# A state-space scan with a gated feed-forward: tokens dealt four to a partition, and a changed order of the first loads and turns

## The chip, the cores and the metric

The kernel runs on one core of a Trainium2 chip. The metric is the device time of one execution in microseconds. A core has five engines with queues of their own: TensorE (PE, matrix products; PEld is its weight load), VectorE (DVE), ScalarE (ACT), GpSimd (POOL) and SyncE (SP), which here only issues transfers.

## The reference

`x` is 2048 tokens of 512 channels, bf16. It is normalised once, and two branches read the result; their product is added to `x`:

```python
xn = _layernorm(x, axis=-1)
# branch A: a diagonal complex recurrence over the tokens
Bu = einsum("bld,pd->blp", xn, ((Lam_bar - 1) / Lam)[:, None] * Bmat)
h  = Lam_bar * h + Bu[:, t, :]                      # for t in 0..2047
s  = 2 * einsum("blp,dp->bld", hseq, Cmat).real + xn * Dskip
# branch B
g  = silu((gelu(xn @ w_gate) * (xn @ w_up)) @ w_down)   # 512 -> 1376 -> 512
return x + s * g
```

## The kernel before, in words

**Tiles.** The tokens are worked in four slabs (`s`) of 512 (`TS`), each of four tiles (`m`) of 128 tokens. Tile `m` of slab `s` holds the tokens `s*512 + m*128 + p`, one to a partition `p` (L195: `x_r`). A slab's `x` comes in one transfer (`load_slab`, L216), but slab 0 comes tile by tile (`load_x`, L221).

**A slab's work.** The normalised tokens `xna` are transposed by a DMA into `xnT`, which has channels on partitions and tokens along the free side. `gate_tile` (L421) makes the products with `w_up` and `w_gate` from it (weights 1376 wide, in three pieces `CH` of 512, 512 and 352), `at_t` turns the gated result by a DMA into `atT`, and `down_pair` (L456) multiplies by `w_down`. `half` (L522) runs the recurrence for half of the states: eight groups of four products give `Bu` in PSUM, ACT copies each into `U` (L534), DVE turns it into a rotating frame (L544), scans along the tokens (L563) and turns back into `hst`, the states in order of time. `y_tile` (L500) multiplies `hst` (as weights, 128 tokens at a time, L482) by `C`, and DVE multiplies by the gate, adds `x` and writes `ot`; SP sends it out in rows (L498). Six PSUM banks (`ring`) go round, two more (`ybank`) serve the turns at the head and the last products.

**The head, slab 0.** Here PE turns tiles 0 to 3 itself, not a DMA. For tile 0 the sum of each token is shared by ACT (L339, the last 128 channels) and DVE (L341, the first 384), DVE subtracts the mean (L343), PE turns it in two pairs (L313), and DVE (L319) and ACT (L321) copy one pair each into `W`, which serves as `xcT`. Tiles 1 to 3 are summed by ACT (L347), centered by DVE (L348), turned by PE (`head_t`, L328) and copied whole by DVE (L330). PE needs `ident` and two little parameter turns too (L588, L589; DVE copies them out in L591). Then come the products with `w_up`, `up_rows(m, k)` (L376): for tile `m` and row block `k` of 128 channels, two products of 128x512, added up over `k` in two banks. The scale of each token (`rs`) is applied when ACT evacuates them (L392). `dummies` (L293) are seven products of constants at the start, `fill(1, 0)` (L299, called in L648) is one more, placed ahead of tile 1's turn.

**Order.** Every step is added to a list by `Plan.add` with what it reads and writes; `ORDER` (L21) is a list of step numbers, written out, and `Plan.run` emits the steps in that order, so it sets the order on each engine's queue. The figures given with a step (cost, landing, rank) don't reach the chip. SP's queue begins with tiles 0, 1 and 2 of `x`, then the row blocks 0, 1 and 2 of `w_up` (the first 1024 columns), tile 3, row block 3, the rest of `w_up`, and `w_gate` (L225 to L234). PE's order at the head is: dummies, turn of tile 0, parameters, filler, turn of tile 1, `up_rows(0,0)`, turn of tile 2, `up_rows(1,0)` and so on.

Of the kernel before, what the change touches and what calls it, by code (L numbers as in the profile page):

```python
# [10 lines left out]
AF = mybir.ActivationFunctionType  # L11
# [7 lines left out]


ORDER = (  # L21
    20, 21, 22, 23, 24, 0, 26, 25, 19, 17, 18, 16, 1, 39, 14, 15, 12, 13, 2, 41, 3, 4, 5, 27, 28, 29, 30, 33, 60, 32, 46, 45, 40, 61, 34, 31, 63, 42,
    65, 62, 64, 69, 68, 66, 67, 70, 71, 72, 73, 35, 36, 37, 50, 51, 52, 54, 48, 53, 49, 57, 56, 58, 137, 38, 6, 43, 44, 147, 7, 79, 76, 82, 74, 80,
    77, 81, 78, 75, 8, 95, 91, 85, 97, 86, 93, 87, 88, 92, 55, 84, 47, 138, 94, 83, 96, 198, 149, 199, 151, 135, 59, 98, 136, 153, 9, 103, 107, 99,
    101, 109, 111, 104, 119, 100, 115, 102, 117, 108, 110, 125, 123, 133, 131, 216, 220, 139, 217, 140, 106, 120, 90, 112, 127, 214, 221, 105, 116,
    134, 154, 218, 150, 113, 126, 118, 124, 89, 215, 114, 128, 219, 122, 141, 148, 121, 143, 222, 223, 129, 130, 142, 152, 10, 11, 155, 160, 164, 179,
    162, 166, 181, 161, 183, 165, 224, 163, 185, 227, 167, 226, 225, 180, 182, 358, 186, 184, 229, 144, 168, 169, 170, 172, 171, 173, 174, 175, 176,
    177, 178, 187, 156, 132, 233, 234, 158, 237, 238, 157, 235, 228, 241, 243, 258, 275, 283, 280, 279, 276, 282, 244, 259, 236, 277, 278, 281, 284,
    285, 159, 239, 245, 296, 264, 247, 240, 246, 292, 260, 242, 200, 201, 202, 265, 302, 262, 297, 311, 293, 261, 298, 248, 303, 317, 307, 204, 188,
    203, 205, 263, 300, 294, 312, 308, 322, 299, 301, 315, 326, 313, 295, 309, 189, 191, 286, 190, 192, 230, 206, 207, 208, 318, 352, 316, 330, 332,  # L30
    232, 231, 305, 304, 327, 341, 209, 210, 211, 310, 324, 314, 328, 331, 323, 337, 290, 325, 339, 345, 287, 329, 288, 289, 333, 146, 320, 193, 212,
    195, 196, 213, 197, 353, 347, 359, 319, 194, 335, 334, 354, 364, 365, 343, 338, 145, 346, 340, 342, 360, 249, 250, 355, 366, 254, 306, 418, 426,
    291, 376, 380, 378, 393, 377, 381, 344, 382, 397, 394, 348, 395, 410, 420, 379, 383, 398, 421, 425, 419, 396, 424, 411, 349, 350, 361, 253, 252,
    369, 251, 256, 257, 357, 266, 267, 336, 414, 435, 415, 370, 436, 375, 255, 321, 356, 362, 351, 416, 443, 450, 412, 444, 423, 417, 445, 399, 422,
    413, 441, 439, 451, 446, 460, 458, 400, 440, 454, 437, 461, 442, 456, 481, 455, 475, 427, 269, 428, 429, 432, 438, 452, 471, 430, 465, 459, 479,
    371, 453, 433, 457, 271, 270, 268, 448, 480, 482, 502, 473, 273, 274, 466, 500, 272, 367, 363, 431, 447, 476, 463, 503, 472, 492, 496, 462, 372,
    486, 493, 501, 497, 474, 373, 484, 384, 385, 388, 386, 387, 467, 368, 434, 537, 477, 523, 494, 519, 478, 498, 487, 495, 524, 499, 525, 526, 520,
    507, 483, 389, 468, 390, 488, 374, 489, 504, 391, 505, 392, 401, 402, 403, 405, 406, 449, 551, 539, 521, 508, 552, 522, 513, 514, 535, 538, 536,
    515, 509, 404, 408, 407, 409, 527, 528, 531, 530, 518, 532, 469, 485, 464, 553, 490, 506, 557, 555, 541, 558, 569, 563, 556, 540, 559, 542, 554,
    565, 561, 567, 564, 578, 619, 562, 560, 574, 570, 624, 625, 576, 620, 584, 575, 568, 566, 580, 577, 591, 585, 599, 582, 589, 583, 597, 579, 593,  # L40
    581, 595, 572, 598, 600, 614, 510, 529, 516, 533, 571, 491, 587, 621, 629, 630, 612, 511, 622, 586, 626, 635, 615, 594, 596, 610, 608, 592, 590,
    604, 606, 636, 613, 607, 609, 605, 611, 534, 543, 544, 617, 601, 545, 573, 517, 627, 512, 602, 631, 470, 649, 616, 547, 548, 546, 549, 550, 637,
    623, 588, 643, 641, 644, 603, 645, 628, 638, 632, 618, 647, 650, 648, 655, 656, 642, 651, 661, 662, 646, 666, 667, 671, 672, 639, 640, 633, 634,
    652, 657, 658, 663, 664, 668, 669, 673, 674, 653, 654, 659, 660, 665, 670, 675,
)


# [33 lines left out]
def kernel(  # L81
# [109 lines left out]
    def dma(eng, issue, land, emit, reads=(), writes=(), **kw):  # L191
        return pl.add(eng, issue, emit, reads, writes, lag=land, **kw)

    TURN, SLAB = (3, 2.28, 1.5), (2, 1.5, 1.0)
    x_r = A_x[0].rearrange("(m p) d -> p m d", p=P)  # L195
    out_td = out[0]
    w_of = {
        "wg": (wg, B_w_gate.rearrange("(k p) f -> p k f", p=P)),
        "wu": (wu, B_w_up.rearrange("(k p) f -> p k f", p=P)),
# [14 lines left out]
               [(nm, k, c) for k in range(k0, k1) for c in range(3) if c0 <= CH[c][0] < c1])  # L214

    def load_slab(s, **kw):  # L216
        dma(SP, 0.8, 4.0, lambda: nc.sync.dma_start(out=x_tok[:, s * M : (s + 1) * M, :], in_=x_r[:, s * M : (s + 1) * M, :]),
            writes=[("x", s, m) for m in range(M)], svc=SLAB, **kw)


    def load_x(m, end, landed):  # L221
        dma_sp(end, landed, lambda: nc.sync.dma_start(out=x_tok[:, m, :], in_=x_r[:, m, :]), [("x", 0, m)])

    W2 = CH[1][1]
    load_x(0, 1.12, 2.92)  # L225
    load_x(1, 1.59, 3.35)
    load_x(2, 2.06, 3.75)
    load_w("wu", 0, 1, 0, W2, 2.53, 5.1)
    load_w("wu", 1, 2, 0, W2, 3.0, 6.3)
    load_w("wu", 2, 3, 0, W2, 3.5, 7.4)  # L230
    load_x(3, 4.0, 7.75)
    load_w("wu", 3, 4, 0, W2, 4.5, 8.7)
    load_w("wu", 0, KT, W2, F, 5.0, 9.9)
    load_w("wg", 0, KT, 0, F, 5.6, 13.7)  # L234
    for ri, src in enumerate((A_B_re, A_B_im)):
# [60 lines left out]
                T.matmul(ybank[j][:] if j < 2 else ring[i][:], lhsT=warm[:, 0:P], rhs=warm, start=True, stop=True)  # L296
        pl.add(PE, k * 0.427, f, [], [("bank", i), ("y", 0), ("y", 1)], lag=0.22, not_before=0.6)

    def fill(k, i):  # L299
        def f():  # L300
            for _ in range(k):
                T.matmul(ring[i][:], lhsT=warm[:, 0:P], rhs=warm, start=True, stop=True)  # L302
        pe(k, 512, f, [], [("bank", i)])

    def head_t(m):

        if m == 0:
# [26 lines left out]
    def center(m):  # L334

        x = x_tok[:, m, :]
        if m == 0:
            c = 3 * P
            acts(D - c, lambda: act(out=junk()[:, 0 : D - c], in_=x[:, c:D], func=AF.Copy, scale=1.0 / D, accum_out=mb[:, 0:1]),  # L339
                 [("x", 0, 0)], ["mb"], ptr=1, rank=400.0)  # L340
            dve(c, lambda: V.tensor_scalar(out=yg[0][:, 0:c], in0=x[:, 0:c], scalar1=1.0 / D, scalar2=None, op0=ALU.mult, op1=ALU.add,  # L341
                                           accum_out=ma[:, 0:1]), [("x", 0, 0)], [("yg", 0, 0), ("ma", 0)], base=0.15, rank=400.0, after=early)
            head.append(dve(512, lambda: V.tensor_scalar(out=xn[0], in0=x, scalar1=ma[:, 0:1], scalar2=mb[:, 0:1], op0=ALU.subtract, op1=ALU.subtract),  # L343
                            [("x", 0, 0), ("ma", 0), "mb"], [("xc", 0, 0), ("xc", 0, 1)], rate=2.3, rank=400.0, after=head[-1:]))
            return
        nmean, key = ma[:, m : m + 1], ("ma", m)
        sums0.append(acts(512, lambda: act(out=junk()[:], in_=x, func=AF.Copy, scale=-1.0 / D, accum_out=nmean), [("x", 0, m)], [key], ptr=2, rank=400.0 - 20 * m))  # L347
        dve(512, lambda: V.tensor_scalar(out=xn[m], in0=x, scalar1=nmean, scalar2=None, op0=ALU.add),  # L348
            [("x", 0, m), key], [("xc", m, 0), ("xc", m, 1)], rate=2.3, rank=330.0 - 20 * m)
# [123 lines left out]
    def y_part(s, m, c0, c1, bank, key, seed, e):  # L473
# [2 lines left out]
        ps = bank[:, 0:w]  # L476
        if seed:
            acts(w, lambda: act(out=ps, in_=sk[s % 2][:, m, c0:c1], func=AF.Copy), [("sk", s % 2, m)], [key])  # L478

        def f():  # L480
            for j in range(2 * NPT):
                T.matmul(ps, lhsT=hst[s % 2][:, j // NPT, j % NPT, m * P : (m + 1) * P], rhs=C2[:, j // NPT, j % NPT, c0:c1],  # L482
                         start=(j == 0 and not seed), stop=(j == 2 * NPT - 1), skip_group_check=True)
        pe(2 * NPT, w, f, [("hst", s % 2, 0), ("hst", s % 2, 1)] + C2S + ([key] if seed else []), [key])
        gi, b = g2s[s, m]
# [2 lines left out]
        else:  # L488
# [3 lines left out]
        o = 2 + m % 2 if s == NS - 1 and m >= M - 2 else m % 2  # L492
        dve(w, lambda: V.tensor_tensor(out=ot[o][:, c0:c1], in0=yg[e][:, c0:c1], in1=x_tok[:, s * M + m, c0:c1], op=ALU.add),  # L493
            [("yg", e, c0), ("x", s, m)], [("ot", o, c0)], rate=2.0)
        mg = s * TS + m * P
        cuts = (0, HD) if (NS - 2, M - 2) <= (s, m) < (NS - 1, M - 2) else (c0,)
        for lo, hi in zip(cuts, (*cuts[1:], c1)):
            dma(SP, 0.35, 1.5, lambda lo=lo, hi=hi: nc.sync.dma_start(out=out_td[mg : mg + P, lo:hi], in_=ot[o][:, lo:hi]), [("ot", o, c0)], [("out", s, m, lo)], svc=(2, 0.4, 0.9))  # L498

    def y_tile(s, m):  # L500
        i = y_n[0] % 2
# [20 lines left out]
    def half(s, h):  # L522
        ui = u_n[0] % NU
        u_n[0] += 1
        for q in range(H2):
            pt = h * H2 + q
            for ri in range(2):
# [3 lines left out]
                    for k in range(KT):  # L531
                        T.matmul(ps[:], lhsT=BT[:, ri, k, pt * P : (pt + 1) * P], rhs=xnT[:, s % 2, :, k, :], start=(k == 0), stop=(k == KT - 1))  # L532
                pe(KT, 512, f, [("BT", ri)] + [("xnT", s % 2, m) for m in range(M)], [("bank", r)])
                acts(512, lambda q=q, ri=ri, ps=ps: act(out=U[ui][:, ri, q, :], in_=ps[:], func=AF.Copy), [("bank", r)], [("U", ui, q, ri)])  # L534
        WQ = [P, 2, 2, H2 * TS]
        hs = slice(h * H2, (h + 1) * H2)
        Uf = U[ui][:].rearrange("p r q t -> p r (q t)")
# [107 lines left out]
    rstd(0, 1)  # L645
    for m in range(1, M):
        norms = rstd(m, m + 1)
    fill(1, 0)  # L648
    head_t(1)
    up_rows(0, 0)  # L650
    up_rows(1, 0)
# [174 lines left out]
```

## Time and profile before

| | |
|---|---|
| three timed runs | 178.66, 179.13, 179.43 us (median 179.13) |
| profiled execution | 178.61 us, span 176.8 us, TensorE clock 1.00 |
| PE busy | 171.7 us (97%), 834 products recorded |
| DVE busy | 156.4 us (88%) |
| ACT busy | 125.1 us (71%) |
| POOL busy | 12.0 us (7%) |
| DMA | 18.66 MB, mean 106 GB/s |

The span runs from the first to the last instruction; what lies around it in the profiled execution is 1.81 us. A group of instructions is named by its line, its engine and what it writes and reads. "PEld" rows are weight loads, which run beside products. "SPq" and "ACTq" rows are instructions that issue a transfer; landing is when the transfer is done.

### The profile page before, as it was taken

The page shows a single profiled execution, that of the slowest core. Times are in us where ns is not written, and L with a number is a line of the kernel's source. Part 1 is how long each engine was busy: PE and PEld are TensorE (multiplying, and loading weights), DVE is VectorE, ACT ScalarE, POOL GpSimd, SP SyncE. Part 2 cuts the span into 40 slices and gives each one's busy share as a digit, 9 for nine tenths or more (in the row PEclk, how much of TensorE's full clock was granted, in tenths as well). Part 3 has the DMA queues.
Part 4 walks back from the last instruction along what each step waited for, and adds up shares of the span by engine and source line. Part 5 has one row for each costly group of instructions (what it writes and reads, how often), then busy time and mean ns, then how long its engine had stood idle before and what let it go on. Part 6 is the DMA issues. An engine that isn't in the chain of part 4 may idle for free.

```text
span 176.8 us, 2414 instructions
## 1 busy us (share of the span) xinstructions
PE 171.7 (97%) x834; PEld 82.7 (47%) x850; DVE 156.4 (88%) x252; ACT 125.1 (71%) x240; POOL 12.0 (7%) x25
## 2 busy tenths in 40 slices
PE   7999999999999999999999999999999999999992
PEld 2555544444455544444445454444444455444451
DVE  3829999999799993999979999899999999999764
ACT  6779999969999999799578855373158618582240
POOL 2462040000200000000040000000000000000000
PEclk9999999999999999999999999999999999999999
DMA  5999999997000809423000075094000007526022
GB/s 141 348 366 222 176 249 279 186 275 150 0 0 2 198 4 177 105 82 59 0 0 6 30 110 121 30 193 85 0 0 0 0 30 157 69 56 139 26 76 76
DMA packets 48083, 18.66 MB, mean 106 GB/s; under 512 B 40296, under 2 KB 47048, under 8 KB 48072
## 3 DMA queue, kind: packets, MB, share of 16 engines
q1 hardware_dynamic: 48048, 18.52, 47.7%
q8 instruction: 6, 0.10, 0.2%
q14 instruction: 5, 0.04, 0.1%
q10 hardware_dynamic: 24, 0.00, 0.0%
HBM read 6.46 MB, written 2.10 MB: 48 GB/s over the span
## 4 chain that ended last, share of the span: by engine, by line
PE 94%; DVE 2%; DMA 1%; issue 1%; DVEq 0%
PE ring L434 31%; PE ring L466 21%; PE ring L532 16%; PE ybank L482 15%; PE ring L402 7%; PE ring L383 3%; DMA x_tok<-in_A_x_dram 1%; PE ybank L383 1%; DVE yg L487 1%; DVE junk L493 1%; PE ybank L328 0%; DVE yg L341 0%; PE ring L313 0%; DVE xna L343 0%; PE ring L302 0%
## 5 line engine op out<-in xcount | busy, mean ns | idle before, releaser
L434 PEld LDWEIGHTS <-xnT 128*128 128x128 bf16 x288 | 28.2, 98 | 28.4
L466 PE MATMUL ring<-wd,atT 128*128 128x512 bf16 (+1 forms) x170 | 38.9, 379 | 0.3
L434 PE MATMUL ring<-wg,xnT 128*128 128x512 bf16 (+1 forms) x143 | 31.4, 357 | 0.1
L434 PE MATMUL ring<-wu,xnT 128*128 128x512 bf16 (+1 forms) x141 | 31.1, 356 | 0.2
L532 PE MATMUL ring<-xnT,BT 128*128 128x512 bf16 x128 | 30.1, 379 | 0.0
L563 DVE TENSOR_TENSOR_SCAN Fs<-rho,ini,W 128x512 bf16<-128x512 f32 x24 | 29.7, 1271 | 0.1
L437 ACT ACTIVATE ub<-ring 128x512 bf16<-128x512 f32 (+1 forms) x36 | 19.2, 555 | 14.1 <-PE ring L434 14.0
L482 PE MATMUL ybank<-C,hst 128*128 128x512 bf16 x116 | 27.3, 379 | 0.2
L466 PEld LDWEIGHTS <-atT 128*128 128x128 bf16 (+1 forms) x176 | 17.2, 98 | 20.8
L534 ACT ACTIVATE U<-ring 128x512 bf16<-128x512 f32 x32 | 18.0, 600 | 6.7 <-PE ring L532 6.7
L437 ACT ACTIVATE gt<-ring 128x512 bf16<-128x512 f32 (+1 forms) x36 | 19.5, 556 | 3.7 <-PE ring L434 3.5
L482 PEld LDWEIGHTS <-hst 128*128 128x128 bf16 x136 | 13.3, 98 | 14.0
L469 ACT ACTIVATE g<-ring 128x512 f32<-128x512 f32 x16 | 9.4, 594 | 14.3 <-PE ring L466 14.2
L532 PEld LDWEIGHTS <-BT 128*128 128x128 bf16 x128 | 12.5, 98 | 14.7
L544 DVE TENSOR_TENSOR Q<-U,tab 128x4096 bf16<-128x4096 bf16 x8 | 18.3, 2290 | 1.0 <-ACT tab L631 0.7
L544 DVE TENSOR_TENSOR Q<-Fs,tab 128x4096 bf16<-128x4096 bf16 x8 | 18.3, 2288 | 0.1
L487 DVE TENSOR_TENSOR yg<-ybank,g 128x512 bf16<-128x512 f32 x15 | 10.2, 685 | 5.4 <-PE ybank L482 5.3
L744 ACT ACTIVATE junk<-x_tok 128x512 bf16<-128x512 bf16 x16 | 10.0, 631 | 0.9 <-DMA x_tok<-in_A_x_dram 0.9
L478 ACT ACTIVATE ybank<-sk 128x512 f32<-128x512 bf16 x15 | 9.1, 605 | 1.7 <-DVE yg L487 1.6
L749 ACT ACTIVATE xna<-x_tok,nb,rs 128x512 bf16<-128x512 bf16 x12 | 9.6, 818 | 0.0
L402 PE MATMUL ring<-wg,W 128*128 128x512 bf16 (+1 forms) x47 | 9.4, 356 | 0.1
L563 DVE TENSOR_TENSOR_SCAN Fs<-rho,W 128x512 bf16<-128x512 f32 x8 | 9.3, 1210 | 0.1
(127 smaller groups left out, 170.5 us busy)
## 6 DMA issues: line engine op xcount, KB each, us to landing
x_tok<-in_A_x_dram SPq DMA_DIRECT2D x3, 512.0 KB, 7.0
wg<-in_B_w_gate_dram SPq DMA_DIRECT2D x1, 1376.0 KB, 8.1
wd<-in_B_w_down_dram SPq DMA_DIRECT2D x1, 1280.0 KB, 7.1
out_dram<-ot SPq DMA_DIRECT2D x10, 128.0 KB, 1.7
wu<-in_B_w_up_dram SPq DMA_DIRECT2D x4, 256.0 KB, 3.6
x_tok<-in_A_x_dram SPq DMA_DIRECT2D x4, 128.0 KB, 2.4
out_dram<-ot SPq DMA_DIRECT2D x8, 64.0 KB, 1.6
wu<-in_B_w_up_dram SPq DMA_DIRECT2D x1, 352.0 KB
```

What stands on the lines that cost most here:

```text
L402: T.matmul(ps[:, 0 : b - a], lhsT=xcT[:, k, m * P : (m + 1) * P], rhs=wt[:, k, a:b], start=(k == 0), stop=(k == KT - 1))
L434: T.matmul(ps[:, 0 : b - a], lhsT=xnT[:, s % 2, m, k, :], rhs=wt[:, k, a:b], start=(k == 0), stop=(k == KT - 1))
L437: acts(b - a, lambda: act(out=dst[:, a:b], in_=ps[:, 0 : b - a], func=AF.Copy if up else AF.Gelu_apprx_tanh), [("bank", r)], [key], table= ...
L466: T.matmul(ps[:], lhsT=atT[:fs, k, m * P : (m + 1) * P], rhs=wd[:fs, k, :], start=(k == 0), stop=(k == NFT - 1))
L482: T.matmul(ps, lhsT=hst[s % 2][:, j // NPT, j % NPT, m * P : (m + 1) * P], rhs=C2[:, j // NPT, j % NPT, c0:c1], start=(j == 0 and not seed ...
L487: dve(w, lambda: V.tensor_tensor(out=yg[e][:, c0:c1], in0=ps, in1=g2[gi][:, b, c0:c1], op=ALU.mult), [key, ("g2", gi, b)], [("yg", e, c0)])
L532: T.matmul(ps[:], lhsT=BT[:, ri, k, pt * P : (pt + 1) * P], rhs=xnT[:, s % 2, :, k, :], start=(k == 0), stop=(k == KT - 1))
L534: acts(512, lambda q=q, ri=ri, ps=ps: act(out=U[ui][:, ri, q, :], in_=ps[:], func=AF.Copy), [("bank", r)], [("U", ui, q, ri)])
L544: dve(4096, lambda: V.tensor_tensor(out=Qf, in0=src.unsqueeze(1).to_broadcast(WQ), in1=table, op=ALU.mult), reads, ["Q"], rate=2.0)
L563: pl.add(DVE, 1.12 if s == 0 else 1.185, lambda ri=ri, q=q, pt=pt, first=first: V.tensor_tensor_scan(out=Fs[:, ri, q, :], data0=rho[:, pt ...
L744: acts(512, lambda i=i, fn=fn, sc=sc, m=m: act(out=junk()[:], in_=x_tok[:, s * M + m, :], func=fn, scale=sc, accum_out=sx[:, s, i, m : m + ...
L749: acts(512, lambda m=m: act(out=xn[m], in_=x_tok[:, s * M + m, :], func=AF.Identity, scale=rs[:, s, m : m + 1], bias=nb[:, s, m : m + 1]), ...
```

## The change

Tokens are dealt four to a partition: tile `m` of slab `s` now holds the tokens `s*512 + 4*p + m`. A slab's transfer so has 4 KB in a row for each partition, and tiles 1 and 2 of slab 0 come in one transfer of 2 KB rows. Since the turned tokens then stand tile by tile, ACT writes `U` with a step of four elements, so that the recurrence runs in order of time as before, and PE loads `hst` as weights with a step of four. Output rows go to every fourth token.

SP's queue becomes: tile 0, tiles 1 and 2 together, row blocks 0, 1 and 2 of `w_up`, tile 3, row block 3, and the rest as before. DVE sums 320 channels of tile 0, ACT 192. The filler product is gone. `ORDER` is a new list. Step by step it differs from the old one at the head only, apart from one more piece of output:

- PE: turn of tile 0, parameters, `up_rows(0,0)`, turn of tile 1, `up_rows(0,1)`, `up_rows(1,0)`, turn of tile 2, `up_rows(1,1)`, `up_rows(2,0)`, then the products that are left; from the turn of tile 3 on it is the old order.
- DVE: the copy of tile 0's pair stands ahead of tile 1's centering, the copy of the parameters behind it; tile 1's copy ahead of tile 2's centering; the statistics of tile 0 ahead of the angles.
- ACT: its copy of tile 0's other pair stands behind tile 1's sum and ahead of tile 2's; tile 3's sum ahead of the sine `sbt`.
- SP: the output of tile 1 of slab 2 is sent in two halves of columns.

```diff
 ORDER = (
...
-    x_r = A_x[0].rearrange("(m p) d -> p m d", p=P)
-    out_td = out[0]
+    x_r, out_td = (t[0].rearrange("(s p m) d -> s p m d", p=P, m=M) for t in (A_x, out))
...
-        dma(SP, 0.8, 4.0, lambda: nc.sync.dma_start(out=x_tok[:, s * M : (s + 1) * M, :], in_=x_r[:, s * M : (s + 1) * M, :]),
+        dma(SP, 0.8, 4.0, lambda: nc.sync.dma_start(out=x_tok[:, s * M : (s + 1) * M, :], in_=x_r[s]),
...
-    load_x(0, 1.12, 2.92)
-    load_x(1, 1.59, 3.35)
-    load_x(2, 2.06, 3.75)
-    load_w("wu", 0, 1, 0, W2, 2.53, 5.1)
-    load_w("wu", 1, 2, 0, W2, 3.0, 6.3)
-    load_w("wu", 2, 3, 0, W2, 3.5, 7.4)
-    load_x(3, 4.0, 7.75)
-    load_w("wu", 3, 4, 0, W2, 4.5, 8.7)
+    load_x(0, 1, 1.12, 2.92)
+    load_x(1, 3, 1.59, 3.65)
+    load_w("wu", 0, 1, 0, W2, 2.06, 4.3)
+    load_w("wu", 1, 2, 0, W2, 2.53, 5.0)
+    load_w("wu", 2, 3, 0, W2, 3.0, 5.7)
+    load_x(3, 4, 3.5, 6.05)
+    load_w("wu", 3, 4, 0, W2, 4.0, 6.8)
...
-            c = 3 * P
+            c = 320
...
+        hv = hst[s % 2][:].rearrange("p r q (t m) -> p r q m t", m=M)
...
-                T.matmul(ps, lhsT=hst[s % 2][:, j // NPT, j % NPT, m * P : (m + 1) * P], rhs=C2[:, j // NPT, j % NPT, c0:c1],
+                T.matmul(ps, lhsT=hv[:, j // NPT, j % NPT, m, :], rhs=C2[:, j // NPT, j % NPT, c0:c1],
...
-        mg = s * TS + m * P
-        cuts = (0, HD) if (NS - 2, M - 2) <= (s, m) < (NS - 1, M - 2) else (c0,)
+        cuts = (0, HD) if (NS - 2, M - 3) <= (s, m) < (NS - 1, M - 2) else (c0,)
...
-                acts(512, lambda q=q, ri=ri, ps=ps: act(out=U[ui][:, ri, q, :], in_=ps[:], func=AF.Copy), [("bank", r)], [("U", ui, q, ri)])
+                acts(512, lambda q=q, ri=ri, ps=ps: act(out=U[ui][:, ri, q, :].rearrange("p (t m) -> p m t", m=M), in_=ps[:].rearrange("p (m t) -> p m t", m=M), func=AF.Copy), [("bank", r)], [("U", ui, q, ri)])
...
-    fill(1, 0)
     head_t(1)
     up_rows(0, 0)
```

## The prediction

> **What bounds the kernel now.** I read the page's shares first (PE busy 97%, DVE 88%, ACT 71%), then the waits by engine, then the timeline of the first 11 us, engine by engine. The waits of PE list two entries only, both before 4.2 us. So I asked for busy time in three stretches (columns: stretch, its length, busy time and count for each engine, granted clock, DMA):
>
> ```profile
> 5.29:10.69 5.40, 5.40 (x28) 2.56 (x28) 3.68 (x13) 3.25 (x10) 3.24 (x7) 1.00 1.03 352
> 10.69:171.90 161.21, 160.37 (x776) 77.13 (x791) 148.24 (x220) 118.30 (x223) 7.40 (x10) 1.00 0.46 96
> 171.90:176.80 4.90, 1.68 (x16) 1.26 (x13) 2.37 (x6) 0.00 (x0) 0.00 (x0) 1.00 0.26 80
> ```
>
> From 5.29 to 171.9 us PE never stops (776 products recorded for 791 loads; the 0.84 us not busy are missing records), at clock 1.00. The end is therefore the start of that dense run, plus a fixed amount of PE work, plus a tail. The head decides:
>
> ```profile
> 4.10 0.48 PE L313 MATMUL ring<-ident,xna 128*128 128x128 bf16 x4 [0.20 <-DVE xna L343]
> ...
> 4.64 0.39 PE L302 MATMUL ring<-const-bfloat16-1.0 128*128 128x512 bf16 x1
> 4.87 0.39 PE L328 MATMUL ybank<-ident,xna 128*128 128x128 bf16 x4
> 5.29 0.59 PE L383 MATMUL ring<-wu,W 128*128 128x512 bf16 x2
> 5.72 0.38 PE L328 MATMUL ybank<-ident,xna 128*128 128x128 bf16 x4
> 5.95 4.91 PE L383 MATMUL ring<-wu,W 128*128 128x512 bf16 x22
> 10.69 0.39 PE L328 MATMUL ybank<-ident,xna 128*128 128x128 bf16 x4
> ```
>
> L313 turns tile 0 (call it T0), the three L328 rows are T1, T2, T3, and L383 are products (m,k) of tile m with row block k of w_up, two each. 22 products in 4.91 us with 0.38 for one: a slot of 0.216 us. A turn of four takes 0.054 x 4 = 0.216. All of T1 to T3 and 24 products lie without a gap because T1 and T2 were issued well before the products that need them. The copies between (DVE):
>
> ```profile
> 2.95 0.55 DVE L341 TENSOR_SCALAR_CACHE_REDUCE yg<-x_tok 128x384 bf16<-128x384 bf16 x1 [1.93 <-DMA x_tok<-in_A_x_dram]
> 3.43 0.08 DVE L341 DVE_READ_ACCUMULATOR yg<-x_tok 128x1 f32 x1
> 3.63 0.41 DVE L343 TENSOR_SCALAR xna<-x_tok,ma,mb 128x512 bf16<-128x512 bf16 x1
> ...
> 4.75 0.17 DVE L591 CAST pf<-ring 128x12 f32<-128x12 bf16 x1 [0.20 <-PE ring L589]
> 4.83 0.28 DVE L319 COPY W<-ring 128x256 bf16<-128x256 bf16 x1
> ...
> 6.15 0.42 DVE L330 COPY W<-ybank 128x512 bf16<-128x512 bf16 x1 [0.36 <-PE ybank L328]
> ```
>
> and the DMA, from issue to landing (issued at 1.17, 1.61 and 2.11 us: tiles 1 and 2 of x, first rows of w_up):
>
> ```profile
> x_tok<-in_A_x_dram SPq DMA_DIRECT2D x1, 128.0 KB, 2.2
> x_tok<-in_A_x_dram SPq DMA_DIRECT2D x1, 128.0 KB, 2.6
> wu<-in_B_w_up_dram SPq DMA_DIRECT2D x1, 256.0 KB, 3.1
> ```
>
> So tile 1 lands at 3.37, tile 2 at 4.2, w_up's first rows at 5.2.
>
> **Tile 0's chain.** DVE's half of the sum goes from 384 to 320 elements. L341 took 0.55 for 384; L599's 196 elements took 0.36 and L279's 512 took 0.69, which is 1.04 ns for one, so 64 fewer are worth 0.07. ACT's half (0.31 for 128, ending 3.36 with its read) grows by 0.05 (L347's 512 took 0.63: 0.83 ns for one) and still ends first, 3.41 against 3.45. T0 is 0.07 earlier: its first pair ends at 4.40 (4.47 now: products of 0.28 starting 4.10 and 4.18). The copy of that pair (L319) now stands ahead of the cast L591 and of tile 1's centering: 4.44 to 4.72, where it was 4.83 to 5.11. PE's load followed that copy by 0.06 and the product by 0.12 more. **(0,0) starts at 4.84 to 4.90 instead of 5.29**, if w_up is there: gain 0.39 to 0.45. The filler L302 goes with it and is inside that gain.
>
> **The queue.** SP's issues are 0.45 apart. Merging tiles 1 and 2 moves w_up's first issue from 2.11 to 1.62. With its own 3.1 it lands at 4.7; the other bound is that it lands as before, 5.2, since the same 384 KB lie ahead of it. I take 4.7: in stretches of 0.2 us the DMA moved 154 GB/s from 3.2 to 3.6 us against 370 to 420 from 4.4 to 5.2, so there was room, and the x packets become 2 KB. The merged tiles land between 3.37 (as tile 1 did) and 4.27 (as tile 2 did); I take 3.7. Tile 1 is then summed by ACT (0.72 from start to read, row L347) by 4.45 and centered (0.35) by 5.06, because DVE holds it behind the copy to 4.72. It is in time for T1 at 5.3 as long as it lands by 4.07; at 4.27 it would cost 0.2. Tile 3, the fourth w_up block and everything after are issued earlier or at the same time; their users (products from 9 us on, T3) have over 1 us.
>
> **Tile 1's turn, now behind (0,0).** Before, T1 was over when (0,0) began; now its 0.216 lies in the dense run: **+0.22**. And in-order PE now meets T1's own latency. T first product to last end 0.39, to DVE 0.04 (T3 ends 11.08, its copy starts 11.12), copy 0.42, to the load 0.06, to the product 0.07 to 0.12 (0.07 from T0, whose first turn shows 0.29 against 0.22): 0.98 to 1.03 before (1,0) can start. Between T1 and (1,0) PE has only (0,1): 0.22 + 0.43 = 0.65. **A gap of 0.33 to 0.38.** The same again: T2 now stands behind (1,0), and only (1,1) lies between it and (2,0). **A second 0.33 to 0.38**; tile 2's centering (ACT sum from 4.83, DVE behind T1's copy, done 6.5) is ready for T2 at 6.8 and adds nothing. From (2,0) on, 16 products remain, with every operand ready.
>
> **Sum of the head:** between -0.45 + 0.22 + 0.66 = +0.43 and -0.39 + 0.22 + 0.76 = +0.59. T3 starts at about 11.2 instead of 10.69. T3's own input: DVE takes tile 0's statistics (0.69 + 0.18) and the angles (2.1 from L593 to L603) ahead of tile 3's centering, done by about 10.7, 0.5 before T3; without that cover each late tenth is a tenth. ACT's first evacuation waits for sbt (angles at 9.9, then 0.37), done before its product. POOL's order is unchanged. I take **+0.5**.
>
> **The stride of four.** Tokens p*4+m make ACT write U at every fourth element and PE read hst so:
>
> ```profile
> L534 ACT ACTIVATE U<-ring x32: 572/597/630, 25.8 to 131.8; 128x512 bf16<-128x512 f32 x32
> L482 PEld LDWEIGHTS <-hst x136: 96/98/99, 64.6 to 173.2; 128*128 128x128 bf16 x136
> ```
>
> No row shows either with a stride. Weight loads: T1's four follow each other every 0.055 us, so a load needs at most that of the loader; below nothing is excluded (a load can't beat being hidden), and even four times as slow it fits the 0.216 slot. Cost zero, up to 128 x (pace - 0.216) beyond that. ACT: zero at one end (one element a cycle either way), and at the other the write takes twice its cycles: 512 elements of L347's 0.83 ns, +0.43 on each of 32. A gain is excluded, the count of elements being the same. I take zero, L534's nearest kin (L437, 555 ns mean, and L469, 594) showing that the place written to hardly matters. The Trainium skill (SBUF — State Buffer, Door 1: The DMA port swizzle) says that two hits on each 16-byte line keep full pace, so bf16 may be strided by up to eight; by it both costs are zero and the sum is the same; no run here shows it yet. The Trainium skill (TensorE: Matmul & The Clock Gate, The mechanism) has a rule against this: weight loads overlap running products only in another row group, so that any slower load would be bare; this trace disagrees, with full-height loads of 98 ns inside gapless 216 ns slots.
>
> **Slabs and outputs.** Slabs of x in 4 KB rows move the same bytes; PE waits for none of them. Output rows of 1 KB now lie 4 KB apart in memory; w_up's 2 KB pieces lie 2752 bytes apart and ran at that full rate. Zero. Tile (2,1)'s output is cut in two: one more issue (0.45) on SP between the transposes at 156.76 and 159.50; the later lands 3.7 after, 163.2, and the last down products need it at 156.98 + 33 x 0.216 = 164.1: covered, 0.9 against 0.45. The tail after PE is unchanged.
>
> **Total.** The profiled execution took 178.61 (span 176.80 and 1.81 around it): 179.1 by its own time. It lay under all three timed runs, so on their median, 179.13, I forecast **179.6** (half a microsecond, 0.3%). A measurement of this kernel can tell about 0.5%, that is 0.9 us, from no change: this is "same".
>
> **Rivals.**
> (a) The gaps don't show, because the turns' latency is shorter than the rows add up to: only -0.42 + 0.22 = -0.2, 178.9. For it: a latency summed from rows can hide an overlap. Against: each link has its own row, and the links of T3 and of the pair copy agree. 14%.
> (b) w_up lands no earlier than before, the DMA being limited by bytes: (0,0) at 5.29, then +0.22 and the two gaps, +0.95: 180.1, on the border. For it: the same bytes ahead. Against: the 154 GB/s. 14%.
> (c) Slower for certain: ACT's strided writes. ACT is full in places (11.97 busy of 12.00 from 38 to 50 us) and seven U copies fall between 72 and 80 us, where a bank comes free only 0.2 to 0.4 us ahead of PE's next load for it (ends of the copies against those loads). It decides from about 0.05 us a copy (7 x 0.05 = 0.35). At the doubled price, 32 x 0.43 = 13.8 of ACT's time, about half absorbed by the 29% in which ACT is idle: +6, 185. 8%.
> (d) Weight loads over the slot: at eight times the pace 0.055, 128 x 0.22 = +28, 207. 3%.
> (e) The change doesn't do what it says, tile 1 and w_up landing as before and the copies no sooner: (0,0) at 5.2 and (1,0) at 6.65, +0.85: 180.0. 4%.
>
> **How the numbers follow.** Forecast 57%, its own range 179.2 to 180.0 with the runs' spread (178.66 to 179.43). No case gives over 0.9 of gain: all that PE loses between T0 and (0,0) now is 0.65 (1.19 less 0.54 of turns and parameters); 5% is left for the spread. Slower by over 0.9: (c), (d), half of (b), a third of (e) and a little of the forecast's edge, 22%. The rest, 73%, is same. The range for 8 in 10 takes in (a), (b) and (e) and leaves (c) and (d): 178.7 to 180.5.
>
> **What would show it.** Right: (0,0) near 4.87; two idle stretches of PE of 0.3 to 0.4 ahead of (1,0) and (2,0); T3 near 11.2; no gap later; U copies at 0.60, loads at 98 ns. Wrong: (0,0) above 5.1 (b), no gaps (a), U copies above 0.65 with PE waiting for ACT (c).

## The result and the profile after

Six runs of the changed kernel took 190.09 us in the median (190.01 to 191.62) against 179.00 for six of the kernel before (178.23 to 179.43): **1.064 times as long**, with a 95% interval of 1.060 to 1.068. The forecast was 179.6, from 178.7 to 180.5. The profiled execution took 190.01, with a span of 188.2 (178.61 and 176.8 before). The ratios here and below leave out runs over 1.5% above the fastest of the same kernel; where runs are counted, all are in.

Three lines of the page: shares, the costliest group of ACT, and the chain that ended last.

```profile
PE 174.4 (93%) x833; PEld 84.1 (45%) x849; DVE 156.6 (83%) x252; ACT 144.8 (77%) x240; POOL 12.0 (6%) x25
...
PE 59%; ACT 33%; issue 2%; DMA 2%; DVE 2%; SPq 0%; DVEq 0%
...
L526 ACT ACTIVATE U<-ring 128x512 bf16<-128x512 f32 x32 | 40.4, 1359 | 3.7 <-PE ring L524 3.7
```

ACT does 19.7 us more with as many instructions, and a third of the chain runs through it. Before, the chain did not touch ACT:

```profile
PE 94%; DVE 2%; DMA 1%; issue 1%; DVEq 0%
```

The copies of `U` (L526, L534 before) went from a median of 597 ns to 1336 ns. 32 x 0.74 is 23.7 us of ACT's time; its busy time grew by less, because records that overlap are counted once.

The stretch of the changed kernel from tile 3's turn (T3) to the start of the last product, and a part of it (columns: stretch, its length, busy time and count for PE, weight loads, DVE, ACT and POOL, clock, DMA share, GB/s):

```profile
11.16:184.71 173.55, 164.49 (x789) 80.27 (x803) 149.88 (x223) 138.03 (x223) 6.72 (x8) 1.00 0.44 90
40.00:60.00 20.00, 15.08 (x68) 6.60 (x68) 14.15 (x22) 19.97 (x34) 1.01 (x1) 1.00 0.30 61
```

The same work, and the same part, of the kernel before:

```profile
10.69:173.31 162.62, 161.78 (x789) 78.40 (x803) 149.57 (x223) 118.30 (x223) 7.40 (x10) 1.00 0.46 96
40.00:60.00 20.00, 19.89 (x100) 9.78 (x100) 18.45 (x28) 19.43 (x39) 1.01 (x1) 1.00 0.28 53
```

The same 789 products take 10.93 longer: 8.22 of it without a product (9.06 against 0.84), and 2.71 of more "busy" PE, because a product ahead of a gap is counted with its whole 0.38 instead of 0.216. Between 40 and 60 us PE idles for a quarter of the time while ACT is never idle. The chief entry of PE's list of waits says on what, and two rows of PE's timeline where:

```profile
PE ring L426 <- ACT U L526: 4.8, 5, 1.3
```

```profile
50.33 1.02 PE L426 MATMUL ring<-wu,xnT 128*128 128x512 bf16 x4 [1.17 <-ACT U L526]
...
53.51 0.76 PE L426 MATMUL ring<-wg,xnT 128*128 128x352 bf16 x4 [1.30 <-ACT U L526]
```

A bank of the ring comes free only when ACT has copied it. Most of the other waits of PE (0.9 for `gt`, 0.7 for `g`, 0.5 for the refill of `ybank`) are for other copies by ACT, which share its queue with those of `U`.

The head of the changed kernel, on PE (L305 is T0, L320 are T1 to T3, L375 the products):

```profile
4.22 0.40 PE L305 MATMUL ring<-ident,xna 128*128 128x128 bf16 x4 [0.42 <-DVE xna L335]
...
4.96 0.59 PE L375 MATMUL ring<-wu,W 128*128 128x512 bf16 x2 [0.21 <-DMA wu<-in_B_w_up_dram]
5.43 0.40 PE L320 MATMUL ybank<-ident,xna 128*128 128x128 bf16 x4
5.77 1.18 PE L375 MATMUL ring<-wu,W 128*128 128x512 bf16 x4
6.79 0.39 PE L320 MATMUL ybank<-ident,xna 128*128 128x128 bf16 x4
7.01 4.31 PE L375 MATMUL ring<-wu,W 128*128 128x512 bf16 x18
11.16 0.39 PE L320 MATMUL ybank<-ident,xna 128*128 128x128 bf16 x4
```

T3 starts 0.47 later than before (10.69). The last sixteen products, after and before:

```profile
183.07 1.91 PE L475 MATMUL ring<-C,hst 128*128 128x256 bf16 x16
```

```profile
171.67 1.91 PE L482 MATMUL ring<-C,hst 128*128 128x256 bf16 x16
```

They start 11.40 later, and so does the last of them (184.71 instead of 173.31); so 0.47 belong to the head and 10.93 to what lies between. After the start of the last product both traces show the same 3.5.

### The profile page after: what moved, and what is told of

It is laid out like the page before. It is cut to its first block, busy times and chain, and to the rows that moved or that the text cites. A ratio compares the mean times of both kernels' runs of the same rounds, so it can differ in the third digit from the quotient of the medians.

```text
span 188.2 us, 2410 instructions
## 1 busy us (share of the span) xinstructions
PE 174.4 (93%) x833; PEld 84.1 (45%) x849; DVE 156.6 (83%) x252; ACT 144.8 (77%) x240; POOL 12.0 (6%) x25
## 3 DMA queue, kind: packets, MB, share of 16 engines
HBM read 6.46 MB, written 2.10 MB: 45 GB/s over the span
## 4 chain that ended last, share of the span: by engine, by line
PE 59%; ACT 33%; issue 2%; DMA 2%; DVE 2%; SPq 0%; DVEq 0%
PE ring L426 23%; ACT U L526 17%; PE ybank L475 13%; PE ring L458 10%; PE ring L394 6%; ACT junk L735 4%; PE ring L524 3%; PE ring L375 3%; ACT g L461 3%; ACT L461 2%; DMA wu<-in_B_w_up_dram 2%; ACT L429 1%; ACT gt L429 1%; ACT xna L740 1%; ACT ub L429 1%
## 5 line engine op out<-in xcount | busy, mean ns | idle before, releaser
L526 ACT ACTIVATE U<-ring 128x512 bf16<-128x512 f32 x32 | 40.4, 1359 | 3.7 <-PE ring L524 3.7
L524 PE MATMUL ring<-xnT,BT 128*128 128x512 bf16 x128 | 30.2, 379 | 0.6 <-ACT gt L429 0.4
L429 ACT ACTIVATE gt<-ring 128x512 bf16<-128x512 f32 (+1 forms) x36 | 20.0, 570 | 2.8 <-PE ring L426 2.6
L475 PEld LDWEIGHTS <-hst 128*128 128x128 bf16 x136 | 15.4, 113 | 12.8 <-issue 0.8
L524 PEld LDWEIGHTS <-BT 128*128 128x128 bf16 x128 | 12.5, 98 | 15.6 <-issue 1.1
L470 ACT ACTIVATE ybank<-sk 128x512 f32<-128x512 bf16 x15 | 9.6, 638 | 1.7 <-DVE yg L480 1.6
```

The source lines that it names most:

```text
L429: acts(b - a, lambda: act(out=dst[:, a:b], in_=ps[:, 0 : b - a], func=AF.Copy if up else AF.Gelu_apprx_tanh), [("bank", r)], [key], table= ...
L475: T.matmul(ps, lhsT=hv[:, j // NPT, j % NPT, m, :], rhs=C2[:, j // NPT, j % NPT, c0:c1], start=(j == 0 and not seed), stop=(j == 2 * NPT - ...
```

## The experiments

The theory after the result: the write of `U` at every fourth element doubles ACT's copies, and their banks come late to PE. The rivals: something else of the new layout (the weights read with a step, slabs in 4 KB rows, outputs spread) costs PE the time, or the head does. Then two questions of mechanism: is it the write or merely any access with a step, and how does it grow with the step? The expectations number their theories afresh each time. "Before" is the kernel before, run on the same chip among the others.

**u_packed: the change without the step in U.** The recurrence then runs over the tokens tile by tile, in another order than that of time.

```diff
-act(out=U[ui][:, ri, q, :].rearrange("p (t m) -> p m t", m=M), in_=ps[:].rearrange("p (m t) -> p m t", m=M), func=AF.Copy)
+act(out=U[ui][:, ri, q, :], in_=ps[:], func=AF.Copy)
```

> The changed kernel with ACT writing U without a step; all else as changed, the weight loads of hst with a step of four among it. It leaves out the return to the order of time, so the scan runs over the tokens tile by tile. Theory (ACT's stepped write is the whole loss behind the head): copies of U at 0.60 us as before, no PE wait after 11.2 us, time 179.0 plus the head's 0.5, 179.5. Rival one (the loss is the weight loads with a step, 113 ns against 98, or the new layout of slabs and outputs): stays at 185 or more. Rival two (both share): 181 to 185.

**u_step_alone: the kernel before, with only that step.** The same edit the other way round, on the kernel before; here too the recurrence meets the tokens in another order.

> The kernel before with ACT's write of U at a step of four as the only edit; its tokens are not dealt so, which puts U in a wrong order of time. Theory: copies of U at 1.34 us, PE waits for ACT as in the changed kernel, 179.0 + 10.6 = 189.6 (the changed kernel's 190.1 less the head's 0.5). Rival (the loss needs the new layout or the weight loads): under 181.

Measured: u_packed 180.30 (5 runs, 179.48 to 180.86), ratio 1.008 (1.004 to 1.011); u_step_alone 189.69, ratio 1.061 (1.058 to 1.063). The copies of `U` in u_packed and in u_step_alone (count: least, median and greatest ns, first and last start in us):

```profile
L526 ACT ACTIVATE U<-ring x32: 573/597/634, 27.9 to 133.9; 128x512 bf16<-128x512 f32 x32
```

```profile
L534 ACT ACTIVATE U<-ring x32: 1294/1340/1459, 25.9 to 142.7; 128x512 bf16<-128x512 f32 x32
```

In u_step_alone 173.56 us pass between T3 and the last product, in the changed kernel 173.55, in the kernel before 162.62. PE's waits for ACT in u_step_alone are those of the changed kernel again, 4.8 us for `U` ahead of the products with `w_up` and `w_gate` and the same smaller ones. One edit carries the whole 10.9. With it gone, in u_packed, the stretch takes 162.6, the rest of the change costs 0.4 to 1.1%, and PE waits for ACT nowhere, though its weights are still loaded with the step:

```profile
L475 PEld LDWEIGHTS <-hst x136: 110/113/116, 66.7 to 175.3; 128*128 128x128 bf16 x136
```

**psum_step: the same tokens, the step on the side that reads.** ACT reads the PSUM bank at every 128th element and writes `U` in a row. This computes the reference.

```diff
-act(out=U[ui][:, ri, q, :].rearrange("p (t m) -> p m t", m=M), in_=ps[:].rearrange("p (m t) -> p m t", m=M), func=AF.Copy)
+act(out=U[ui][:, ri, q, :].rearrange("p (t m) -> p t m", m=M), in_=ps[:].rearrange("p (m t) -> p t m", m=M), func=AF.Copy)
```

> The changed kernel with the step on the other side of the same copy: ACT reads PSUM with a step of 128 elements and writes U without one; it computes what the reference asks. Theory (the price is on the written side): copies at 0.60 us, 179.5. Rival (any step in an evacuation costs ACT the same, or a step in PSUM more): copies at 1.3 us or more, 190 or more.

Measured: 180.64 (10 runs), ratio 1.008 (1.004 to 1.011), and copies as without any step:

```profile
L526 ACT ACTIVATE U<-ring x32: 577/597/632, 27.9 to 133.9; 128x512 bf16<-128x512 f32 x32
```

A step of 512 bytes on the PSUM side costs nothing; the price belongs to the write. The ten runs fall apart into two groups, 179.14 to 179.73 (4) and 180.62 to 181.36 (6), which no expectation had. That is taken up below.

**u_forms: eight ways to write U.** In the kernel before, the copies of `U` take eight forms by turns, four copies each; the order of the tokens is not kept. In `steps(u, m)` each element lies `m` elements behind the one before, in `runs(u, 4, j)` stretches of `j` neighbours are written four stretches apart. In short:

```diff
+def steps(u, m): out=u.rearrange("p (t m) -> p m t", m=m), in_=ps[:].rearrange("p (m t) -> p m t", m=m)
+def runs(u, m, j): out=u.rearrange("p (t m j) -> p m t j", m=m, j=j), in_ likewise in a row
+by turns: plain; steps 2, 4, 8, 32, 128; runs(u, 4, 2); runs(u, 4, 8)
```

> The kernel before with the copies of U written in eight forms in turn, four copies of each, one line of code a form: no step, steps of 2, 4, 8, 32 and 128 elements, runs of 2 elements every 8, runs of 8 elements every 32. U is in a wrong order of time. Read by the copy's duration. Theory one (each element that does not follow its neighbour costs 1.44 ns more): 0.60; all steps from 2 to 128 at 1.34; runs of 2 at 0.97, runs of 8 at 0.69. Theory two (what counts is how often a 16-byte line is touched, two touches being enough): 2 and 4 alike and cheap, 8 and up dear; but step 4 at 1.34 already speaks against it. Theory three (bytes passed over set the price): it grows with the step, 2 at about 0.85, 8 at over 2.

Measured, in that order (plain; 2, 4, 8, 32, 128; runs of 2; runs of 8):

```profile
L540 ACT ACTIVATE U<-ring x4: 581/594/622, 25.7 to 125.1; 128x512 bf16<-128x512 f32 x4
L542 ACT ACTIVATE U<-ring x4: 737/746/782, 26.2 to 128.9; 128x512 bf16<-128x512 f32 x4
L544 ACT ACTIVATE U<-ring x4: 1310/1316/1319, 27.9 to 129.5; 128x512 bf16<-128x512 f32 x4
L546 ACT ACTIVATE U<-ring x4: 2439/2453/2570, 29.6 to 133.1; 128x512 bf16<-128x512 f32 x4
L548 ACT ACTIVATE U<-ring x4: 2416/2447/2777, 33.1 to 135.9; 128x512 bf16<-128x512 f32 x4
L550 ACT ACTIVATE U<-ring x4: 2454/2616/2782, 35.0 to 138.8; 128x512 bf16<-128x512 f32 x4
L552 ACT ACTIVATE U<-ring x4: 627/632/979, 38.2 to 146.5; 128x512 bf16<-128x512 f32 x4
L554 ACT ACTIVATE U<-ring x4: 591/594/616, 38.7 to 147.0; 128x512 bf16<-128x512 f32 x4
```

No theory had all the numbers. The price grows with the step up to eight, and little or nothing beyond (2447 ns at 32, 2616 at 128). Count how often a write enters a stretch of eight elements (16 bytes): 128 times at step 2, 256 at step 4, 512 at step 8 and beyond. From 2 to 4 the time grows by 0.570 for 128 entries, from 4 to 8 by 1.137 for 256: 4.45 and 4.44 ns an entry. So a step of four costs 0.176 + 256 x 4.45 ns = 1.32. This holds for single elements at steps 2 to 8 only: in a row (64 entries) it would give 0.46, and 0.594 was measured, and pairs of neighbours escape it, as they too enter 256 times and take 0.63. Why they do is not settled by these rows; that single 2-byte elements four or more apart are dear, and 4-byte pairs eight elements apart are not, is what they show. So the count of entries is a fit, not a shown cause. The Trainium skill (SBUF — State Buffer, Door 1: The DMA port swizzle) lets bf16 stride by up to eight for nothing, because two accesses to each 16-byte line suffice; this trace disagrees for ACT's writes: step 4 makes two to each line and took 1316 ns, step 2 makes four and took 746, against 594.

**pe_step: the step on PE's moving operand.** The change without the step in `U` (as u_packed), and PE takes the turned tokens in order of time, so that neighbours of its moving operand lie 1 KB apart. This computes the reference.

```diff
-rhs=xnT[:, s % 2, :, k, :]
+rhs=xnT[:, s % 2, :, k, :].rearrange("p m t -> p t m")
```

> The third place for the return to the order of time: PE takes the tokens of xnT in order of time, four tiles in turn, as the moving operand of the 128 products that make Bu (two-byte elements 1 KB apart), so that PSUM and U need no step; it computes what the reference asks. If the moving side pays nothing, 179.5 and a slot of 0.22 us for these products; if it pays as ACT's written side did (2.45 us for 512 elements in lines of their own), each slot grows and the time is 179.5 + 128 x (slot - 0.22), 206 at a slot of 0.43.

Measured: 277.5 us in one run. The 128 products of L524:

```profile
L524 PE MATMUL ring<-xnT,BT x128: 1024/1042/1051, 26.6 to 229.5; 128*128 128x512 bf16 x128
```

They follow each other 0.865 us apart instead of 0.216, four times as slow, so 128 x 0.65 = 83 of the 98 us more. Some of the rest is other products that fell into stretches of half clock and follow each other 0.427 apart there. Of the three places tried for the return to the order of time, this is the dearest, and the PSUM read the only one found free.

**no_fill: the kernel before without its filler product.** In psum_step's profiled execution, one of the later group (180.72), the first products follow each other at half pace:

```profile
5.37 1.01 PE L375 MATMUL ring<-wu,W 128*128 128x512 bf16 x2 [0.41 <-DMA wu<-in_B_w_up_dram]
...
6.60 1.91 PE L375 MATMUL ring<-wu,W 128*128 128x512 bf16 x4
...
8.64 0.59 PE L375 MATMUL ring<-wu,W 128*128 128x512 bf16 x2
```

Two products take 1.01 at 5.37 and 0.59 at 8.64: 0.427 and 0.216 apart. In the trace the records of a full granted clock begin at 8.5 us in that execution, at 3.6 in the changed kernel's and at 4.3 in that of the kernel before. The change dropped one product (0.22 of work) in just that time. Theory: the filler makes PE reach its full clock early.

```diff
-    fill(1, 0)
```

> The kernel before without its one filler product, nothing else. In the profiles of u_packed and psum_step products were issued 0.43 us apart until 8.6 us, against 0.22 from 4.4 us on before; their runs fall into two groups, about 179.3 and 180.9. Theory (a full clock is granted at the end of a stretch of time in which PE was busy enough, and the filler counts): without it the times fall into two groups here too, 178.6 and about 180.3, and the median moves toward the second. Rival (the filler only costs its 0.2 us and the clock hangs on something else, such as the later loads): all runs near 178.6, one group.

Measured: median 178.84, as before's own (29 runs), ratio 1.003 (0.999 to 1.006). But 4 of 12 runs took 180.68 to 181.22, against 1 of 29 of the kernel before. The groups came as expected, the median did not move. That the group near 181 is the one with the late clock is read from other kernels: of the profiled executions under 182 us, the four that took 180.7 or more had a full clock only from 8.5 us on or later (psum_step, u_packed, psum_fill, psum_fill_order), the others, of 179.5 and less, by 6.6. No execution of no_fill near 181 has a profile, and the counts are small.

**psum_fill: psum_step with the filler, behind the parameters' turn; psum_fill_order: also with the third row block of w_up ahead**, so that the products (0,2) and (1,2) stand in the two gaps of the head.

```diff
 psum_fill, in the head (and its step in ORDER behind the parameters' turn)
+    fill(1, 0)
     head_t(1)
 psum_fill_order, PE's steps in ORDER: (0,0), T1, (0,1), ...
-(1,0), T2, (1,1), (2,0), (0,2), (1,2)
+(0,2), (1,0), T2, (1,1), (1,2), (2,0)
```

> psum_step (changed kernel, ACT reading PSUM with the step) with the filler product back, between the parameters' turn and tile 0's products, where PE waited for w_up. Theory of the clock: one group of runs near 179.3, the head's 0.5 over before. Rival (the new head loses its clock anyway, by the wait for w_up and the gaps ahead of (1,0) and (2,0)): still two groups, median 180.5.

> psum_fill with two pairs of products moved on PE alone: (0,2) ahead of (1,0) and (1,2) ahead of (2,0), so that PE has 0.43 us more to do in each of the two gaps of the head (0.5 and 0.6 us in the changed kernel's trace). Theory (the turns' latency makes those gaps): T3 starts at 10.7 to 10.8 instead of 11.2, the time is that of before, 178.8. Rival (w_up's third block isn't there by then, landing at 6.3): gaps move ahead of (0,2), 179.1 to 179.3.

Measured: psum_fill 179.32 (12 runs), ratio 1.005 (1.003 to 1.007), 1 of 12 above 180.5, where psum_step, on another chip, had 6 of 10. psum_fill_order 179.45 (14 runs, 2 above 181), ratio 1.003 (1.001 to 1.005); it did not get below the kernel before. The profiled executions of both had the late clock (full from 9.4 and 9.0), so each was profiled a second time:

> psum_fill again, for a trace in which the full clock comes by about 5 us, as in 11 of its 12 timed runs. Theory: T3 at 11.1 to 11.2, gaps of 0.3 to 0.6 us ahead of (1,0) and (2,0), 179.3.

> psum_fill_order again, for the same reason: it gained nothing over psum_fill, 179.45 against 179.32. If the turns' latency made the gaps they are gone here and something earlier is late; if w_up's third block is late, the gap stands ahead of (0,2) and T3 at 11.1.

These two took 179.27 and 179.01, with a full clock from 5.0. T3 starts at 11.32 in the first and at 11.04 in the second: filling the gaps is worth 0.28 in these two profiles, which the medians don't show. It is less than hoped. The gaps were 0.25 each in the first, and 0.14 and 0.25 in the changed kernel's trace, not the 0.5 and 0.6 of the expectation; a gap of 0.17 now stands ahead of (0,2), whose rows of `w_up` come third and land at 6.46; and (0,0) starts at 5.2 in both.

**layout_alone: the kernel before with the dealt layout only**: loads and outputs by the new rows, weights with a step of four, `U` by psum_step's read; the old order, the single transfers and the filler stay.

```diff
+    x_r, out_td = (t[0].rearrange("(s p m) d -> s p m d", p=P, m=M) for t in (A_x, out))
+        hv = hst[s % 2][:].rearrange("p r q (t m) -> p r q m t", m=M)
+act(out=U[ui][:, ri, q, :].rearrange("p (t m) -> p t m", m=M), in_=ps[:].rearrange("p (m t) -> p t m", m=M), func=AF.Copy)
```

> The kernel before, its order and its loads one by one, with the tokens dealt four to a partition and the return to the order of time made by ACT reading PSUM with a step (free in psum_step); output rows and weight loads of hst with the step too. psum_fill runs 0.5 us over before; this tells layout from order. Theory (the 0.5 is the head's order: tile 1's turn in the dense run and the two gaps): 178.8, T3 at 10.7. Rival (the first tile, read in rows 4 KB apart, lands 0.15 to 0.2 later, 3.1 against 2.95, and that is part of it): 179.0, T0 at 4.2 to 4.3.

Measured: 178.96 (12 runs) against 179.01 (18), ratio 1.001 (0.999 to 1.002): no price that these runs show. From T3 to the last product its profile takes 162.6, as those of psum_step, u_packed and the kernel before do: behind the head the layout is free. In the head the rival's sign is there: tile 0 was used at 3.17 and T0 began at 4.31, for 2.95 and 4.10 before. T3 came at 11.58 in this one profile (179.51), whose full clock began only at 6.53, so what the later tile 0 costs by itself is not told. By difference, what is left of psum_fill's 0.5% belongs to the head's order and transfers.

## Why the prediction was wrong

**The step that failed** is the one on the stride of four: "ACT: zero at one end [...] and at the other the write takes twice its cycles [...] I take zero". It named both ends and chose the wrong one. The row it leaned on (L437 and L469, that the place written to hardly matters) told of other places, all written in a row; no row of the trace before had a step, so nothing there pulled towards the cheap end. The measured +0.74 a copy lies even beyond the dear end of +0.43: the bound came from doubling the time for one element, while the steps in u_forms fit a price for each entry into a 16-byte stretch, 256 of them here. Rival (c) had the mechanism, with the full ACT between 38 and 50 us and the banks that come free just in time, and held 8%. Its share was right too: it took about half of ACT's added time to reach PE, and 10.9 of 23.7 (46%) did. With the measured price it would have given 32 x 0.74 x 0.5 = 11.8 instead of +6.

The other steps:

- **Weight loads with a step: right.** 98 became 113 ns, hidden; layout_alone and psum_step have them and take 162.6 from T3 to the last product, as before. Rival (d) is out.
- **The sum of the head: right (+0.47 for +0.5), its terms only in part.** (0,0) came at 4.96, for a forecast of 4.84 to 4.90, since `w_up`'s first rows landed at 4.92, not 4.7: -0.33 instead of about -0.42. T1 in the dense run costs its 0.22. The gaps came out smaller, 0.14 ahead of (1,0) and 0.25 ahead of (2,0) for 0.33 to 0.38 each, because from a turn to the product that needs it 0.91 and 0.90 pass, not 0.98 to 1.03; for the first, 0.04 ahead of T1 and 0.10 ahead of (0,1) had already taken a part of the wait. -0.33 + 0.22 + 0.53 is 0.42, and 0.05 is not accounted for. A smaller gain and smaller gaps cancel: that the sum fits so well is in part luck. The landing of `w_up` also differs from one profile to the next, 4.78 to 5.54 in eight with the new queue and 4.89 to 5.71 in five with the old, so one profile of each does not tell what the earlier issue is worth.
- **The merged tiles** landed at about 4.25, not 3.7, near the upper bound of 4.27, and tile 0's own sum began at 3.13 instead of 2.95, so that T0 is later (4.22), not 0.07 earlier. Rivals (a), (b) and (e) were about this; none decides, beside 10.9.
- **The filler "is inside that gain": incomplete.** For the order of the head it is. That the same product bears on how often PE has its full clock early was missing (times above 180.5: 4 of 12 without it and 1 of 29 with it in no_fill's comparison, 6 of 10 in psum_step and 1 of 12 in psum_fill). Between an early and a late clock lie 1.7 us of span in psum_fill's two profiles (177.5 and 179.2) and 2.2 in psum_fill_order's (177.2 and 179.4).
- **Slabs, outputs, the cut of tile (2,1)'s output, the tail: right**, by layout_alone, by the equal stretch from T3 to the last product, and by the equal 3.5 after its start. The rows of tile 0, 4 KB apart too, were left out of that step: they arrive later, at a price that is not told.

With the write mended, psum_step's earlier group (179.14 to 179.73) is what the forecast of 179.6 was made for. That is an agreement of size; its chances were wrong all the same, as they gave 8% to what happened.

## What to carry to other kernels

A layout that suits the DMA moves its step to some engine: find where the step lands, and prefer the side that measured free (here ACT's read of PSUM) to the write of single 2-byte elements. An operation of which the trace has no row with that access pattern deserves a chance near its dear end, above all on an engine that the profile shows full for whole stretches. Judge the price by a bound on the worst pattern (here 4.1 times the plain copy at step 8), not by "twice the cycles".

## What the runs showed of the hardware

- ACT's write of 512 bf16 elements to SBUF: 0.594 us in a row, 0.746, 1.316 and 2.453 at steps 2, 4 and 8, 2.447 and 2.616 at 32 and 128; 0.632 for pairs. Its read of PSUM at every 128th f32 element: 0.597.
- PE's moving operand with neighbours 1 KB apart: 0.865 us a product instead of 0.216. Though PE shows no idle time, the granted clock falls to half there for long stretches (mean 0.814), and the products keep their 0.865 at both clocks (38 distances at full, 75 at half), where the other products of that run go from 0.216 to 0.427 apart. So the clock of the array does not set that pace; that the delivery of the operand does is the reading that is left.
- The instant of the full clock varies from run to run, from 3.6 to 9.8 us over the profiles of this case, and the records of the clock last whole multiples of 3.413 us (174.08 is 51 of them, 170.67 is 50). By the Trainium skill (TensorE: Matmul & The Clock Gate, What's actually happening) the clock is judged in free-running windows of 3413 ns; the trace agrees.
- With rows of 1 KB lying 4 KB apart, tile 0 was used at 3.13 to 3.26 us in nine traces, in the old layout at 2.84 to 2.95 in four.
